# Landmark attention, a dense layer and routed experts in one kernel: one list of work for attention and dense stage, gates kept in SBUF, w2 loaded into w_in's buffers

## The chip, the cores and the metric

One core of one Trainium2 chip runs the whole computation as one program. Its engines are TensorE (PE, the matrix products; PEld is its weight load), VectorE (DVE), ScalarE (ACT), GpSimd (POOL) and SyncE (SP, which here issues nearly all DMAs). They run side by side, each through its own list of instructions in order, and wait for one another by semaphores. The metric is the device time of the program in microseconds. It is given as the median of several timed runs; a profile is of one more execution.

## What is computed

```python
def _attn_ref(q, k, v):                       # 4 batches, 8 heads, 576 tokens, 64 columns
    q_lm, k_lm = means of 18 neighbours of q, k     # 32 landmarks
    A, Bm, C = sm(q, k_lm), sm(q_lm, k_lm), sm(q_lm, k)
    Z = Bm.T / (norm1 * norminf + 1e-6)
    for _ in range(6):
        Z = 2 * Z - Z @ Bm @ Z
    return A @ Z @ C @ v

def _moe_ref(x, w_in, w_out):                 # 2304 x 512, d_ff 2048
    h = x @ w_in
    return (h * clip(h + 3, 0, 6) / 6) @ w_out

def _moe2_ref(x, w_gate, w1, w2, capacity):   # 8 experts, F 1024, capacity 576
    expert_idx = argmax(x @ w_gate); gate_w = softmax at expert_idx
    # a token gets gate_w * (relu(x @ w1[e]) @ w2[e]) while its expert has room, else 0
```

w_in and w_out come as 64-bit floats and are turned into 32-bit ones on the chip. Products are made with operands split in two (hi and lo, three products for one).

## The kernel before

**Three stages.** The attention stage works on eight units (four batches, two groups of four heads): landmark means (`turn_qk`), `landmark_scores`, `norms`, `gather_v`, `newton` (the inverse, which ends with the copy to `xt`), and `token_scores`, which writes `at`. Attention and dense layer are folded: `project` multiplies `xt` with a quarter of w_in (VV, tile `vv`, the mark "V"), and `first` multiplies that with `at`. So the dense stage needs no attention output. Its width of 2048 is cut in four quarters (`fq`), its tokens in eight blocks of 288 (two to a batch). `first` makes four tiles of 128 hidden rows, evicted by ACT and DVE into r, and split into ghi (ACT) and glo (POOL, or DVE); `second` multiplies them with a quarter of w_out and adds the result to `yacc`. Blocks 6 and 7 (the last batch) get no `second`: their r goes to DRAM (`r_d`), and their gate logits come from r times w_out times w_gate (`gate_weights`, `logits`). `route` picks each token's expert; for the inputs here each of the first three batches goes to one expert, so three units run through `run_unit` (`up_layer`, then `down_layer` in chunks of 128 tokens). What is only for other inputs stands behind a branch that is not taken.

**The order of work.** Each engine's list is fixed when the program is built. `Order` (line 25) is a planner: every step is an `op` with an engine, a cost in us, what it waits for (`after`), buffers that it takes, and a rank. It takes the step that can start first, and among those that can start within a short look-ahead the lowest rank. For a DMA it counts 2 us and the KB given (`DMA_KB`). The instructions are then issued in that order, and no engine ever goes out of order.

**Two plans.** The attention stage is one run of the planner (lines 775 to 791): loads in the order `LOADS`, the attention steps, and `moe_begin`, which puts the firsts and seconds of quarter 0 for blocks 0 to 5 between them, one first and one second of the block before in turn; when it ends block 5's seconds are still open. The attention's memory is then closed, and the dense stage is a second run (lines 966 to 991): the rest of the projections, the conversions of w_out's quarters 1 to 3 (`convert`; quarter 1 of w_in has been loaded in the first plan), `gate_weights`, `logits`, `route` for batches 0, 1 and 3 (`ROUTED`), the store of `yacc` (`store_y`), the load and split of unit 0's w1 (`w1_first`, chunks `raw_e`), and `dense`, which takes firsts and seconds in the order `BLOCKS`, blocks 6 and 7 among them. Batch 2 is routed behind the plan (line 992). PSUM's eight banks are shared out anew between the plans (`open_rest`).

**Gates and w2.** `route` works on tokens in chunks of 96: six transposes (line 871), then some fifteen small DVE operations. It stores a batch's 576 gates to DRAM (line 920, 4 bytes each) and `load_gates` reads them back in chunks of 128 at the head of each unit. Unit 0's w2 is loaded in four quarters while its up-layer runs (`fetch2`, tile `raw`), and split there by ACT and POOL (`split2`), in ACT's list between the evictions of `up_layer`.

Of the kernel before, what the change touches and what calls it, by code (L numbers as in the profile page):

```python
# [125 lines left out]
def nystrom_moe_kernel(ctx, tc, qt, kt, v, w_in, w_out, w_gate, w1, w2, capacity, out, dims, dbg=None):  # L126
# [17 lines left out]
    RN = HB // RT  # L144
# [4 lines left out]

    LAST = NBLK - 2  # L150
    NST = (UNIT + P - 1) // P
# [10 lines left out]
    gate_d = dp.tile([(B - 1) * S], F32, name="gate_d")  # L162
# [7 lines left out]
    for e in range(2):  # L170
# [8 lines left out]
    upper = kp.tile([RT, RT], BF16, name="upper")  # L179
    nc.gpsimd.memset(upper, 1.0)  # L180
    nc.gpsimd.affine_select(out=upper, in_=upper, compare_op=ALU.is_gt, fill=0.0,
                            base=0, pattern=[[1, RT]], channel_multiplier=-1)
    ones_b = kp.tile([RT, RT], BF16, name="ones_b")
    nc.gpsimd.memset(ones_b, 1.0)
    down = kp.tile([RT, E], F32, name="down")
    base_e = kp.tile([RT, E], F32, name="base_e")
    for e in range(E):
        nc.gpsimd.memset(down[:, e:e + 1], float(E - e))
        nc.gpsimd.memset(base_e[:, e:e + 1], float(e * NT))
    half = kp.tile([P, 1], F32, name="half")  # L190
    nc.gpsimd.memset(half, 0.5)
    cap_i = cp.tile([RT, 2], I32, name="cap_i")
    nc.scalar.dma_start(cap_i, capacity.bitcast(I32).to_broadcast([RT, 2]))
    cap_f = kp.tile([RT, 1], F32, name="cap_f")
# [4 lines left out]
    chosen = kp.tile([RT, NBLK, RN, E], F32, name="chosen")  # L199
# [1152 lines left out]
```

## Time and profile before

| | us |
|---|---|
| median of 3 timed runs (lowest, highest) | 562.46 (562.12, 562.86) |
| the profiled execution: its own time | 564.0 |
| its span, first to last instruction | 562.2 |
| first dense product on PE | 63.58 |
| first product of expert unit 0 | 399.16 |
| mean clock of TensorE, of full | 0.991 |

Times in the trace are counted from the first instruction. A line such as L423 is a line of the kernel above; "out<-in" names the tiles. Matmuls are pipelined, so a group's mean is longer than the distance between two of them, and the chain shows the pace better. In the views of windows the columns are the width, then for each engine its busy us and number of instructions, the share of TensorE's full clock that was granted, the mean busy share of the 16 DMA engines, and the GB/s that they moved. What stands in square brackets at the end of a timeline row is the engine's idle time before it and who ended that.

### The profile page before, as it was taken

How to read it: one execution, taken by the hardware profiler on the slowest of the kernel's cores; microseconds unless marked ns; L12 is line 12 of the kernel's file. 1: busy time of each engine (PE TensorE's matmuls, PEld its weight loads, DVE VectorE, ACT ScalarE, POOL GpSimd, SP SyncE). 2: the span in 40 equal slices, each digit the busy share in tenths (PEclk: the TensorE clock that was granted, in tenths of full speed). 3: DMA queues.
4: the chain of work that ended last, by engine and by line, in shares of the span. 5: the costliest groups of instructions: out<-in, count | busy, mean ns of one | idle time of the engine just before them, and what ended most of it. 6: DMA issues, size and time to landing. Idle time of an engine off the chain costs nothing.

```text
span 562.2 us, 12046 instructions
## 1 busy us (share of the span) xinstructions
PE 536.0 (95%) x4827; PEld 462.7 (82%) x4827; DVE 286.9 (51%) x691; ACT 285.2 (51%) x663; POOL 201.1 (36%) x236
## 2 busy tenths in 40 slices
PE   8888999999889999999999999997889999999995
PEld 6655688799577999889979899997787899689884
DVE  2798977823388886558554473566524012302200
ACT  3786787754467555356454354534157152643210
POOL 4486565833124521033223023321064370733000
PEclk9999999999899999999999999998999999999999
DMA  8964435110182542302100010244394910500011
GB/s 297 340 224 161 164 118 165 38 40 1 45 260 92 148 127 81 107 2 97 44 22 0 33 55 1 85 160 95 85 334 127 332 43 0 178 37 21 1 49 42
DMA packets 27841, 59.75 MB, mean 106 GB/s; under 512 B 6528, under 2 KB 11136, under 8 KB 27776
## 3 DMA queue, kind: packets, MB, share of 16 engines
q1 hardware_dynamic: 27136, 58.87, 31.7%
q8 instruction: 40, 0.66, 0.5%
q14 instruction: 25, 0.20, 0.1%
q10 hardware_dynamic: 640, 0.02, 0.1%
HBM read 45.90 MB, written 12.98 MB: 105 GB/s over the span
## 4 chain that ended last, share of the span: by engine, by line
PE 81%; DVE 8%; DMA 5%; ACT 4%; issue 1%; POOL 0%; SPq 0%; ACTq 0%; DVEq 0%; POOLq 0%
PE py L423 26%; PE ph L379 16%; PE ps_o L1074 12%; PE ps_h L1056 12%; PE pn L722 2%; PE pb L359 2%; PE ps_o L1081 2%; DMA raw_e<-in_moe_w 2%; PE warm L769 2%; DMA gate<-gate_d 1%; PE ps_v L359 1%; DVE sums L546 1%; DMA raw<-in_moe_w_out 1%; DMA raw<-in_moe_w_in 1%; PE pw L705 1%
## 5 line engine op out<-in xcount | busy, mean ns | idle before, releaser
L423 PE MATMUL py<-ghi,wo 128*128 128x288 f32 x768 | 160.0, 301 | 3.0 <-DVE yacc L435 3.0
L423 PEld LDWEIGHTS py<-ghi,wo 128*128 128x128 f32 x768 | 124.4, 190 | 8.5 <-issue 5.1
L409 POOL TENSOR_TENSOR glo<-r,ghi 128x288 fp32r<-128x288 f32 x86 | 70.2, 822 | 168.7 <-ACT ghi L402 122.1
L379 PE MATMUL ph<-at,vv 128*128 128x288 f32 x768 | 122.8, 302 | 1.7 <-DVE r L392 1.6
L379 PEld LDWEIGHTS ph<-at,vv 128*128 128x128 f32 x768 | 107.5, 189 | 12.4 <-DVE r L392 6.9
L423 PE MATMUL py<-glo,wo 128*128 128x288 f32 x384 | 114.2, 297 | 0.4 <-DVE glo L406 0.4
L390 ACT ACTIVATE r<-ph,half 128x288 f32<-128x288 f32 x128 | 63.3, 501 | 79.8 <-PE ph L379 60.1
L392 DVE SCALAR_TENSOR_TENSOR r<-r,ph 128x288 f32<-128x288 f32 x128 | 57.0, 451 | 54.8 <-ACT r L390 54.1
L423 PEld LDWEIGHTS py<-glo,wo 128*128 128x128 f32 x384 | 72.8, 189 | 1.1 <-DVE glo L406 0.9
L1062 DVE SCALAR_TENSOR_TENSOR hT<-ps_h,hT 128x288 fp32r<-128x288 f32 x48 | 21.8, 457 | 94.3 <-ACT hT L1059 63.0
L1074 PE MATMUL ps_o<-w2s,hT 128*128 128x512 f32 x288 | 66.2, 391 | 0.0
L1074 PEld LDWEIGHTS ps_o<-w2s,hT 128*128 128x128 f32 x288 | 53.8, 188 | 13.6 <-issue 2.4
L402 ACT ACTIVATE ghi<-r 128x288 fp32r<-128x288 f32 x96 | 42.1, 445 | 24.6 <-DVE r L392 23.7
L1019 POOL TENSOR_TENSOR w2s<-raw,w2s 128x512 fp32r<-128x512 f32 x24 | 30.1, 1291 | 41.7 <-ACT w2s L1018 41.7
L435 DVE TENSOR_TENSOR yacc<-py,yacc 128x288 f32<-128x288 f32 x72 | 32.6, 453 | 22.0 <-PE py L423 21.8
L1059 ACT ACTIVATE hT<-ps_h 128x288 fp32r<-128x288 f32 x48 | 19.7, 411 | 42.6 <-PE ps_h L1056 42.6
L277 POOL TENSOR_TENSOR wo<-cvt,wo 128x512 fp32r<-128x512 f32 x16 | 22.1, 1381 | 38.1 <-ACT wo L275 33.1
L1085 ACT ACTIVATE rows_o<-ps_o,gate 128x512 f32<-128x512 f32 x12 | 8.3, 691 | 41.5 <-PE ps_o L1074 39.2
L722 PE MATMUL pn<-yy 128*128 128x192 f32 (+1 forms) x112 | 27.5, 339 | 1.4 <-DVE vv L366 0.7
L1056 PE MATMUL ps_h<-at,vv 128*128 128x288 f32 x192 | 26.3, 296 | 2.1 <-DVE hT L1062 2.1
L1056 PEld LDWEIGHTS ps_h<-at,vv 128*128 128x128 f32 x192 | 25.6, 188 | 2.4 <-DVE hT L1062 2.3
L1056 PE MATMUL ps_h<-at,wo 128*128 128x288 f32 x192 | 25.8, 294 | 0.0
(207 smaller groups left out, 759.9 us busy)
## 6 DMA issues: line engine op xcount, KB each, us to landing
raw<-in_moe_w_out SPq DMA_DIRECT2D x16, 512.0 KB, 3.7
raw<-in_moe_w_in SPq DMA_DIRECT2D x16, 512.0 KB, 4.2
raw<-in_moe_w SPq DMA_DIRECT2D x8, 1024.0 KB, 7.4
r_d<-r SPq DMA_DIRECT2D x32, 144.0 KB, 1.8
vm<-in_v SPq DMA_DIRECT2D x8, 512.0 KB, 7.3
qT<-in_q SPq DMA_DIRECT2D x6, 576.0 KB, 5.2
qT<-in_k SPq DMA_DIRECT2D x6, 576.0 KB, 6.0
yt_d<-yacc SPq DMA_DIRECT2D x12, 288.0 KB, 2.5
```

The costliest lines, as they stand in the source:

```text
L277: nc.gpsimd.tensor_tensor(dst[1], xf, dst[0].bitcast(F32), op=ALU.subtract)
L379: nc.tensor.matmul(ph, lhsT=vv[pair][g][a][:, b, f * P:(f + 1) * P], rhs=at[pair][c][:, g, tok], start=n == 0, stop=n == 3 * NG - 1)
L390: nc.scalar.activation(r, ph, AF.Relu, bias=half, scale=1.0 / 6.0)
L392: nc.vector.scalar_tensor_tensor(r, r, 1.0, ph, op0=ALU.min, op1=ALU.mult)
L402: nc.scalar.activation(ghi, r, AF.Copy)
L409: nc.gpsimd.tensor_tensor(glo, r, ghi.bitcast(F32), op=ALU.subtract)
L423: nc.tensor.matmul(py, lhsT=w[a][:, f, d * P:(d + 1) * P], rhs=gh[f][c], start=f == 0 and n == 0, stop=f == NF - 1 and n == 2)
L435: nc.vector.tensor_tensor(y, py, y, op=ALU.add)
L722: nc.tensor.matmul(pn[:, cols], lhsT=yy[:, 0:P], rhs=yy[:, cols], start=True, stop=True)
L1019: nc.gpsimd.tensor_tensor(dst[1], src, dst[0].bitcast(F32), op=ALU.subtract)
L1056: nc.tensor.matmul(ps, lhsT=w1s[i % 2](f // NF, a, kk)[:, fs], rhs=xT[c][:, kk, cols], start=n == 0, stop=n == 3 * KC - 1)
L1074: nc.tensor.matmul(ps, lhsT=hT[a][:, f, cols], rhs=w2s[c][:, f, :], start=n == 0, stop=n == 3 * FC - 1)
```

## The change

- One plan for attention and dense stage. `moe_begin` and `dense` become three streams that the planner mixes freely: `firsts`, `seconds` (both in the order of the new `BLOCKS`, blocks 0 to 5 only) and `lasts` (blocks 6 and 7). The projections of quarter 1 for batches 0 and 1 are in the plan from the start. When all eight units have left `xt` and `at`, `room2` closes the attention's memory and adds what was the second plan.
- New ranks and a new order of loads; `store_y` and the store of r count their KB in the planner.
- `route` works in chunks of 128 (five transposes), and `down_layer` takes the gate straight from `prob` in SBUF. The DRAM tile of the gates, its stores and its loads are gone.
- w_in's two buffers stay for the whole program. `w2_first` loads unit 0's raw w2 into them, in two halves, once batch 0 is routed and w_in is used up; `raw2` is these buffers, also for the later units.

The core of the diff (the attention functions move out of a `with` block, otherwise as they were):

```diff
-LOADS = [('out', 3), ('qk', 1), ('out', 1), ('qk', 0), ('v', 1), ('qk', 2), ('out', 2), ('v', 0), ('qk', 4), ('out', 0), ('v', 2), ('qk', 3), ('in', 1), ('in', 0), ('qk', 5), ('in', 2), ('in', 3), ('v', 7), ('v', 4), ('v', 3), ('qk', 7), ('in', 6), ('v', 5), ('in', 5), ('in', 4), ('v', 6), ('qk', 6), ('in', 7)]
+LOADS = [('out', 3), ('qk', 1), ('out', 1), ('qk', 0), ('v', 1), ('qk', 2), ('out', 2), ('v', 0), ('qk', 4), ('out', 0), ('v', 2), ('qk', 3), ('in', 1), ('v', 7), ('in', 0), ('qk', 5), ('in', 2), ('in', 3), ('v', 4), ('v', 3), ('in', 4), ('v', 5), ('in', 6), ('qk', 7), ('v', 6), ('qk', 6), ('in', 7), ('in', 5)]
-RANK = {'in': -39.11, 'out': -156.08, 'next': 307.67, 'C': 7.14, 'A': 103.25, 'B': 97.9, 'Cv': 62.1, 'Z': -35.93, 'sum': 18.24, 'V': 10.16, 'g': 140.36, 'w': -82.95, 'first': -102.38, 'second': 135.87, 'evict': 86.86, 'late': -2.87, 'fill': 29.53, 'out2': 9.76, 'in2': -36.7, 'wg2': 9.18, 'logit': -6.56, 'route': -21.37, 'unit': 17.29}
+RANK = {'in': -210.42, 'out': -85.49, 'next': 285.02, 'C': 2.83, 'A': 122.98, 'B': 61.74, 'Cv': 43.88, 'Z': -40.91, 'sum': 31.39, 'V': -10.32, 'g': 126.04, 'w': -260.15, 'first': -222.88, 'second': 248.13, 'evict': 67.29, 'late': 0.01, 'fill': -117.25, 'out2': 171.78, 'in2': -214.46, 'wg2': 107.62, 'logit': -20.62, 'route': -202.82, 'ahead': 42.91, 'unit2': 100.03, 'unit': 65.75, 'first2': 135.87, 'second2': 135.87, 'V2': 122.79}
-BLOCKS = ((0, 1, 2, 3, 4, 5, 6, 7), (0, 3, 1, 5, 7, 2, 6, 4), (0, 4, 6, 2, 7, 5, 3, 1), (6, 7, 3, 1, 0, 2, 5, 4))
+BLOCKS = ((0, 0), (0, 1), (0, 2), (0, 3), (0, 4), (0, 5), (1, 0), (1, 1), (1, 4), (1, 2), (1, 3), (1, 5), (2, 0), (2, 2), (2, 1), (2, 5), (2, 3), (2, 4), (3, 2), (3, 0), (3, 1), (3, 3), (3, 4), (3, 5))
 ROUTED = (0, 1, 3)
-BANKS = {"h": (3, 4, 1), "y": (5, 2), "m": (0, 6, 7)}
...
-    gate_d = dp.tile([(B - 1) * S], F32, name="gate_d")
...
-    wi = [sp.tile([P, KC, QW], F32, name=f"wi{i}") for i in range(2)]
+    wi = [kp.tile([P, KC, QW], F32, name=f"wi{i}") for i in range(2)]
...
-        rest = state["alone"]
+        rest = fq > 1 or fq == 1 and out
...
-            yield op("SP", 0.35)
+            yield op("SP", 0.35, 144)
             nc.sync.dma_start(r_d[blk - LAST, fq * NF + f], r)
...
+    def firsts():
+
+        for fq, blk in BLOCKS:
+            state["g", fq, blk] = {}
+            yield op(None, after=[("V", fq, blk // 2, g) for g in range(NG)] + (
+                [("at", blk // 2, g) for g in range(NG)] if fq == 0 else []))
+            for f in range(NF):
+                order.spawn(RANK["evict"], first(fq, blk, f, state["g", fq, blk]))
+                yield op(None, after=[("queued", "first", fq, blk, f)])
+
+    def seconds():
+
+        for fq, blk in BLOCKS:
+            for d in range(KC):
+                yield op(None, after=[("first", fq, blk, NF - 1)])
+                order.spawn(RANK["evict"] + 0.5, second(fq, blk, d, state["g", fq, blk]))
+                yield op(None, after=[("queued", "second", fq, blk, d)])
+
+    def lasts():
+
+        for fq in range(NQ):
+            for blk in range(LAST, NBLK):
+                state["r", fq, blk] = {}
+                yield op(None, after=[(*what, B - 1, g) for what in (("V", fq), ("at",)) for g in range(NG)] + [("room2",)])
...
+        ps = [spare(i, [P, n, KC, M], "ps_lt") for i, n in zip(ids, (NST - 1, 1))]
+        cols = lt.rearrange("p n t -> p (n t)")
+        for t in range(NST):
+            o = ps[t // (NST - 1)][0:size(t), t % (NST - 1)]
+            nc.tensor.transpose(o.rearrange("p d c -> p (d c)"), cols[:, t * P:t * P + size(t)], ident)
...
-        if b < B - 1:
-            yield op("SP", 0.4, rank=RANK["late"])
-            nc.sync.dma_start(gate_d[b * S:(b + 1) * S].rearrange("(c j p) -> p c j", p=RT, c=2), prob[:, 2 * b:2 * b + 2, :, 0])
...
-            yield op("SP", 0.35, 0.0, {}, [("y", NQ - 1, 2 * b + n, d) for n in range(2)])
+            yield op("SP", 0.35, 288, {}, [("y", NQ - 1, 2 * b + n, d) for n in range(2)])
...
+    def w2_first(a):
+        yield op("SP", 0.45, 1024, {}, [("pick", 0), ("gated", NQ - 1)] + [("V", NQ - 1, b, g) for b in range(B) for g in range(NG)])
+        nc.sync.dma_start(wi[a], w2[bass.ds(state["ex", 0], 1), a * 4 * P:(a + 1) * 4 * P, :].rearrange("o (k p) f -> p (o k) f", p=P))
+
+    def room2():
+
+        yield op(None, after=[("x", b, g) for b in range(B) for g in range(NG)] + [
+            ("at", b, g) for b in range(B) for g in range(NG)] + [("gated", 0)])
+        order.spawn(0.0, room3())
+
+    def room3():
+
+        yield op(None, take={"b": 2})
+        att.close()
...
+        order.mark(("room2",))
+        order.spawn(RANK["late"], clear())
...
-                    order.spawn(RANK["fill"] + fq + pair * 0.1 + g * 0.01, again(fq, pair, g))
+                    if fq > 1 or pair:
+                        order.spawn(RANK["V2"] + fq + pair * 0.1 + g * 0.01, again(fq, pair, g))
...
+        for g in range(NG):
+            order.spawn(RANK["ahead"] + g, again(1, 0, g))
+        order.spawn(9.0, room())
+        order.spawn(9.0, room2())
...
+        for stream in (firsts, seconds, lasts):
+            order.spawn(-1.0, stream())
...
-        raw2 = [up.tile([P, FC // 2, DM], F32, name=f"raw2{i}") for i in range(2)]
+        raw2 = wi
...
-            load_gates(i)
             for f in range(FC):
                 hi, lo = up_layer(i, f)
                 split2(f)
-                if i == 0 and f < 3:
-                    with tc.issue_after(hi):
-                        fetch2(state["ex", 0], (f + 1,), 4)
...
-                down_layer(k, gates[i][0:size(k), k:k + 1], lambda ro: nc.sync.dma_start(out[rows, :], ro))
+                down_layer(k, prob[0:size(k), i, k, :], lambda ro: nc.sync.dma_start(out[rows, :], ro))
...
-        fetch2(state["ex", 0], (0,), 4)
```

## Rows read from the trace of the kernel before

**Rows 1.** The page, part 1: busy us, share, instructions of each engine.

```profile
PE 536.0 (95%) x4827; PEld 462.7 (82%) x4827; DVE 286.9 (51%) x691; ACT 285.2 (51%) x663; POOL 201.1 (36%) x236
```

**Rows 2.** Busy time per 10 us: width, PE, PEld, DVE, ACT, POOL, clock, DMA share, GB/s.

```profile
140.00:150.00 10.00, 7.93 (x58) 4.77 (x57) 3.08 (x6) 4.34 (x9) 1.48 (x2) 0.83 0.00 0
...
160.00:170.00 10.00, 8.27 (x75) 6.12 (x74) 8.16 (x17) 5.93 (x12) 3.61 (x3) 1.00 0.80 241
170.00:180.00 10.00, 9.57 (x163) 7.13 (x160) 7.78 (x16) 8.58 (x19) 4.91 (x5) 1.00 0.32 105
...
380.00:390.00 10.00, 6.83 (x46) 6.33 (x45) 6.22 (x19) 4.66 (x10) 2.10 (x3) 0.94 0.29 64
390.00:400.00 10.00, 8.91 (x64) 7.69 (x64) 4.79 (x11) 1.87 (x4) 0.00 (x0) 0.89 0.52 123
...
410.00:420.00 10.00, 7.93 (x60) 7.71 (x59) 3.02 (x7) 7.05 (x19) 7.86 (x7) 1.00 1.02 390
```

**Rows 3.** PE's waits over the whole span: us in total, times, longest.

```profile
PE ps_h L1056 <- DVE hT L1062: 2.1, 1, 2.1
PE ph L379 <- DVE r L392: 1.6, 1, 1.6
```

**Rows 4.** The chain in order of time, dense stage: start us, us, what.

```profile
140.60 1.59 PE py L423 x12
...
158.52 1.60 PE py L423 x12
...
202.81 0.80 PE ph L379 x6
...
311.06 1.02 PE pb L359 x16
312.08 1.00 PE ph L379 x6
...
366.63 0.33 PE ps_lt L871 x3
```

**Rows 5.** Timeline of ACT and POOL at the join: start us, us, what.

```profile
137.66 0.44 ACT L748 ACTIVATE xt<-px 64x64 f32<-64x64 f32 x2
...
145.97 0.68 ACT L231 ACTIVATE cvt<-raw 128x512 f32<-128x512 f32 x1
...
168.27 1.49 POOL L277 TENSOR_TENSOR wo<-cvt,wo 128x512 fp32r<-128x512 f32 x1 [4.86 <-ACT wo L275]
```

**Rows 6.** Timeline of ACT and PE near the end of the dense stage.

```profile
384.92 0.63 ACT L952 ACTIVATE vv<-raw_e 128x512 fp32r<-128x512 f32 x1 [3.79 <-DMA raw_e<-in_moe_w]
...
387.43 0.53 PE L423 MATMUL py<-ghi,wo 128*128 128x288 f32 x2 [3.03 <-DVE yacc L435]
```

**Rows 7.** Timeline of SP's queue there: issues of w1's chunks and of gates.

```profile
373.59 0.95 SPq L945 DMA_DIRECT2D raw_e<-in_moe_w  x2
376.00 0.33 SPq L920 DMA_DIRECT2D gate_d<-prob  x1
```

**Rows 8.** DMA issues: count, KB each, median us to landing.

```profile
gate_d<-prob SPq DMA_DIRECT2D x3, 2.2 KB, 8.4
```

**Rows 9.** The view of Rows 2, in 2 us.

```profile
382.00:384.00 2.00, 2.00 (x18) 2.00 (x17) 0.46 (x1) 0.00 (x0) 0.00 (x0) 1.00 0.00 0
```

**Rows 10.** Timeline of DVE and PE: last split of w1, first product of unit 0.

```profile
394.56 0.68 DVE L954 TENSOR_TENSOR wo<-raw_e,wo 128x512 fp32r<-128x512 f32 x1
...
399.16 1.82 PE L1056 MATMUL ps_h<-at,vv 128*128 128x288 f32 x12
```

**Rows 11.** The chain in order of time, in the expert stage.

```profile
403.02 8.40 DMA gate<-gate_d
...
453.71 25.43 PE ps_h L1056 x192
```

**Rows 12.** The view of Rows 2, before the dense products begin.

```profile
40.00:50.00 10.00, 8.02 (x226) 4.73 (x225) 9.17 (x22) 5.93 (x20) 9.59 (x16) 1.00 0.45 143
50.00:60.00 10.00, 9.20 (x111) 5.96 (x109) 8.61 (x24) 6.88 (x20) 4.23 (x4) 1.00 0.50 167
```

More of the change, by code (lines that the diff above doesn't have):

```diff
@@ L368, in project, with again @@
             order.mark(("V", fq, 2 * pair + b, g))
+    def again(fq, pair, g):
+        yield op(None, after=[("in", fq, k) for k in (2 * g, 2 * g + 1)] + [
+            ("first", fq - 1, 4 * pair + n, f) for n in range(4) for f in range(NF)])
+        yield from project(fq, pair, g)
     def first(fq, blk, f, out):
-        yield op("PE", 0.8, None, {"h": 1}, rank=RANK["second"])
+        state["cold"] = False
+        yield op("PE", 0.8, None, {"h": 1}, rank=RANK["fill"] if blk >= LAST else RANK["first2"])
         pair, b = blk // 4, blk // 2 % 2
@@ new lines, in nystrom_moe_kernel, with issue, load_qk @@
+    ap = att.enter_context(tc.tile_pool(name="att", bufs=2))
+    late = att.enter_context(tc.tile_pool(name="late", bufs=2))
+    main = 4 * P
+    NB = S // M
+    units = [dict(b=b, g=g, n=b * NG + g, q={}, rank=2.0 * b + RANK["g"] * g) for b in range(B) for g in range(NG)]
+    turn = [0]
+    def issue():
+        turn[0] += 1
+        return [("issue", turn[0] - 1)] if turn[0] > 1 else []
+    def load_qk(c, i):
+        n = c["n"]
+        yield op("SP", 0.45, 576, {"qT": 1} if n >= NG else {}, issue())
+        if n < NG:
+            qT = yacc[0][2 * n + i].rearrange("p (h t) -> p h t", h=4)
+        else:
+            qT = lp.tile([P, 4, HB], F32, tag="qT", name="qT", bufs=QT_BUFS)
+        c["q"][i] = qT
+        nc.sync.dma_start(qT, (qt, kt)[i][n])
+        order.mark(("qk", n, i))
@@ new lines, in newton @@
+    def newton(c):
+        st, yy = c["st"], c["yy"]
+        for it in range(7):
+            cols = slice(0 if it < 6 else P, P + D)
+            yield op("PE", 0.34 if it < 6 else 0.16, 0.27, {"s": 1})
+            i_s, pn = taken([P, P + D], "pn")
+            nc.tensor.matmul(pn[:, cols], lhsT=yy[:, 0:P], rhs=yy[:, cols], start=True, stop=True)
+            if it == 6:
+                break
+            yield op("DVE" if it else "ACT", 0.28, None, {"yy": 1})
+            yn = late.tile([P, P + D], F32, tag="yy", name="yy", bufs=4)
+            if it == 0:
+                nc.scalar.activation(yn, pn, AF.Copy, scale=st[:, 10:11])
+            else:
+                nc.vector.scalar_tensor_tensor(yn, yy, 2.0, pn, op0=ALU.mult, op1=ALU.subtract)
@@ new lines, in newton @@
+        xx = late.tile([P, 2, D], F32, tag="xx", name="xx")
+        nc.vector.scalar_tensor_tensor(xx, x6, 2.0, p6, op0=ALU.mult, op1=ALU.subtract)
+        order.give("s", 1, [i_s])
+        order.give("yy")
+        yield op("PE", 0.11, None, {"s": 1})
+        b, g, odd = c["b"], c["g"], c["b"] % 2
+        i_s, px = taken([P, 2, 2, M], "px")
+        nc.tensor.transpose(px.rearrange("p j h l -> p (j h l)"), xx.rearrange("p i d -> p (i d)"), ident)
+        yield op("ACT", 0.35)
+        order.give("xx")
@@ new lines, in newton, with values, room @@
+        for hh in range(2):
+            pr = slice(hh * D, (hh + 1) * D)
+            nc.scalar.activation(xt[pr, (b // 2) * NG + g, odd], px[pr, :, hh ^ odd, :], AF.Copy)
+        order.give("s", 1, [i_s])
+        order.mark(("x", b, g))
+    def values(b, g):
+        yield op(None, after=[("x", b, g)] + [("in", 0, k) for k in (2 * g, 2 * g + 1)] + ([("room",)] if b >= 2 else []))
+        yield from project(0, b // 2, g, (b % 2,))
+    def room():
+        yield op(None, after=[("scored", n) for n in range(2 * B)])
+        load.close()
+        s1 = early.enter_context(tc.tile_pool(name="slots1", bufs=1, side=RIGHT, reuse_waits="tile"))
+        vv[1] = [[s1.tile([P, 2, QW], F32R, name=f"vv1{g}{i}") for i in range(2)] for g in range(NG)]
+        yacc[1] = [s1.tile([P, S], F32, name=f"yacc1{d}") for d in range(KC)]
+        order.mark(("room",))
@@ L994, in nystrom_moe_kernel @@
             for step in route(b):
[L995 removed]
+                order.got.update(s=list(range(step[3].get("s", 0))) if step else [])
     early.close()
@@ L1014, in nystrom_moe_kernel @@
         xraw = rx[:, 0:KC * S].rearrange("p (k n) -> p k n", k=KC)
-        gates = [up.tile([P, NST], F32, name=f"gate{i}") for i in range(B - 1)]
         def split(dst, src):
```

737 lines of the change are left out of this document (318 added, 419 removed).

## Prediction

> **What bounds the kernel now.** I read four views, in this order. The page's busy times say that PE is the bound: 536.0 of 562.2 us, the next engine at 287 [rows 1]. Its products are the same before and after, so this case is about the 26 us in which PE stands, about time at half clock, and about what would fill either. The windows of 10 us then show where PE stands once the dense products have begun (before that it waits for loads and for the attention chain): it is full from 80 us on but for three places [rows 2]. At the join of the two plans (140 to 180 us) it is idle for 2.07 + 1.73 + 0.43 = 4.2 us, and the clock of the first window is 0.83, so 1.7 us of pace are lost too. At the end of the dense stage (380 to 400) it is idle for 3.17 + 1.09 = 4.3 us, with clocks 0.94 and 0.89, again 0.6 + 1.1 = 1.7 us. In the first expert unit (410 to 420) it is idle for 2.07 us at full clock. The last store at the very end is not touched. PE's waits name the engine that was late: DVE's hT (2.1) in unit 0, DVE's r (1.6) at the join [rows 3]; the wait at the dense end is traced below. The chain in order of time gives the pace of single products, and the timelines what stands ahead of a late one.
>
> **Work on PE.** A first product (6 matmuls) takes 0.80 us and a second one (12) 1.60 [rows 4]. There are 128 firsts and 96 seconds on both sides, as many projections, the same gate sums, the same three expert units. Only route changes: five transposes for six. Three take 0.33 us [rows 4], so four routes save 4 x 0.11 = 0.4 us. Its DVE work is as many operations on 40 elements a row instead of 48; I cost it at nothing, since DVE is half idle.
>
> **The join.** Today nothing of the second plan (projections for quarter 1, blocks 6 and 7, w_out of quarter 1) may stand in a queue ahead of the first plan's last operation. The last xt is copied at 137.66, ACT's first conversion of w_out's next quarter starts at 145.97, and the last lo half of those four chunks is done at 168.27 + 1.49 = 169.8 [rows 5]: 23.8 us of conversion, and 8.3 us lost ahead of it. After the change it may start when the attention has ended. What can PE do without it? The first plan's last products end at 142.2, and four seconds are left over (the last of them at 158.52): 6.4 us [rows 4]. New in that supply are two projections for quarter 1 (1.02 us, and 0.20 for the slower product behind, [rows 4]: 2.4) and the eight firsts whose g buffers exist (6.4): to 142.2 + 6.4 + 2.4 + 6.4 = 157.4. Once the attention has ended come blocks 6 and 7 (eight firsts: 6.4) and two projections of one batch (half of 1.02 each: 1.0): to 164.8. The conversion would end at 137.7 + about 1.5 + 23.8 = 163.0. So the 4.2 + 1.7 = 5.9 us can close with 1.8 us to spare. I leave 1.6 us in, because the wait on DVE's r [rows 3] came while conversions and evictions shared DVE (82% busy in 160 to 170 [rows 2]), and they still will. Gain 4.3; bounds 0 and 5.9.
>
> **The dense end.** ACT waits 3.79 us for a chunk of w1, the r and yacc operations queue behind it, and PE then stands for 3.03 us [rows 6]. The two chunks had been issued from 373.59 on; the next issue on SP's queue, at 376.00, is the store of 576 gates of 4 bytes [rows 7]. These stores take 8.4 us to land, for 2.2 KB [rows 8], and in 382 to 384 the DMA engines move nothing while this one and the chunk are still out [rows 9]. With the gates kept in SBUF no such store exists. Also the plan now counts the bytes of the yt and r stores (288 and 144 KB), so ACT's copies of w1 should be placed where the data is. Idle 3.17 and clock 1.7 can close: 4.9. The other 1.09 us stay, since batch 2 is still routed behind the plan. Against it comes something new: 2 MB of w2, whose place on SP's queue can be ahead of w1's second half. Its cost: the last split of w1 ends at 394.56 + 0.68 = 395.2, PE needs it at 399.16 [rows 10], a slack of 3.9, plus the 3.8 no longer waited, less the 4.9 by which PE comes earlier: 2.8 us. 2 MB at the 390 GB/s of the fullest window [rows 2] take 5.4 us: all ahead costs 2.6, half ahead nothing. I take 0.6. Gain 4.3; bounds 0 and 4.9.
>
> The Trainium skill (DMA: Bandwidth & Descriptors, Anatomy of one DMA — SWDGE (gpsimd) path) puts a small transfer at a fixed 2.0 us or so and says that most of it is the receipt of the write. By an estimate from that page a gate store would land in about 2 us, nothing would be held up by it, and taking the gates' store away would be worth nothing at this place. The trace disagrees for these stores, which run on another queue than the page's fit: 8.4 us [rows 8].
>
> **Unit 0.** The chain stands 8.40 us on a load of gates at 403.02 [rows 11], issued between the quarters of w2; behind it ACT splits w2, and the eviction of hT comes late. With w2 already in w_in's buffers the 2.07 us close. The up-layers of later units, which never wait, take 25.43 us [rows 11], and w2 is needed whole only after one. Gain 2.1; bounds 0 and 2.1.
>
> **Before the dense products.** From 40 to 60 us PE is idle for 1.98 + 0.80 = 2.8 us [rows 12]. Loads and ranks are reordered here (w_in's conversion higher, the eighth v ahead of w_in's first chunk), and the trace of before can't show what that does. Products that begin earlier gain about these 2.8 us at most, and as much may be lost by a later begin; I take 0.
>
> **Sum.** 4.3 + 4.3 + 2.1 + 0.4 = 11.1 us. The profiled execution took 564.0 us (span 562.2 and 1.8 around it), 1.5 above the median of the runs shown, 562.46; from it 552.9, and from the median 551.4, which I predict. With every hole closed and the early gain it is 562.46 - 5.9 - 4.9 - 2.1 - 0.4 - 2.8 = 546.4.
>
> **Rivals.**
> *More closes than I grant, or products begin early:* 546.4 to 549. For it: one plan sees all the work at once. Against: it must be right about every wait.
> *The join's hole stays*, because conversion waits for its turn on ACT and DVE behind evictions (its rank goes from 10 to 172, so it is taken last): 551.4 + 4.3 = 555.7. DVE's 82% speaks for it, the time to spare against.
> *w2 goes ahead of w1*, with the yt stores of batch 1 too (1.15 MB, 3.0 us): 2.6 to 5.6 us and 1.7 of clock, less the 0.6 granted: 555 to 558.
> *w1 was late for another reason than the gates*, and the end hole stays whole: 551.4 + 4.3 = 555.7.
> *Slower: the attention ends late.* With one list, products and attention compete all along on PE, and quarter 1's conversion, blocks 6 and 7 and the memory for them wait for the last xt. Beyond the 1.8 us to spare every us of delay is a us in which PE stands, and one clock dip of 1.7 comes with it. The gain of 11.1 + 1.6 = 12.7 (the old hole gone whole) is used up, and 1.1 more, when the last xt comes 1.8 + 12.7 + 1.1 - 1.7 = 13.9 us later, at about 151.6; at 157 the time is 569. Against it: for the second head group the offset plus the rank falls from 104 to 85 (Newton), 147 to 129 (landmark scores) and 150 to 116 (values), against 135.87 for products, so the chain to xt is favoured more than before. For it: token scores move back, and the two v buffers are shared with the eighth v earlier.
>
> **Chances.** The forecast (549 to 554) 0.50; more closes 0.11; the join stays 0.12; w2 ahead of w1 0.10; another reason 0.04; holes that only move, 0.03; the attention late 0.10. The range holds all but the last two and the edges: 545.5 to 558.5. A change of 0.2% (1.1 us) is about what a measurement of this kernel can tell from none. Faster 0.87, same 0.03, slower 0.10.
>
> **What would show it.** Right: no idle of PE over 1 us in a window between 80 us and the end of the dense stage, except about 1 us at the last route; no half clock there; ACT not waiting for a chunk of w1; 25.5 us for the up-layer of unit 0; the expert stage's end as before. The prediction is wrong if the last xt is later than about 141 us, if PE stands for over 2 us at the join, if w1's chunks land behind w2, or if the first dense product moves by several us.

## The result and the profile after

The changed kernel takes 543.33 us (median of 4 runs, 542.96 to 543.89), the kernel before in the same session 562.66 (562.12 to 563.10): a ratio of 0.9658, with an interval from 0.9641 to 0.9674. The gain is 19.3 us where 11.1 were forecast, and the time lies 2.2 us below the range. The profiled execution took 543.89 us (span 542.2). In later comparisons, on other chips, the kernel before gave medians of 565.9 to 566.8 (single executions 562 to 571), while the changed one stayed at 543.8: a ratio of 0.9608 and a gain of 22.7 us there. So the kernels made from the changed one are held against its own 543.3 to 543.8, and spans of profiled executions against spans.

The page of the changed kernel, its parts 1 and 4 (busy us of each engine; shares of the chain that ended last):

```profile
PE 528.7 (98%) x4826; PEld 459.1 (85%) x4826; DVE 288.6 (53%) x691; ACT 281.6 (52%) x666; POOL 202.7 (37%) x232
...
PE 87%; DVE 7%; ACT 2%; DMA 1%; issue 1%; POOL 0%; SPq 0%; ACTq 0%; POOLq 0%
```

PE was busy for 536.0 us of 562.2 [rows 1]; now it is for 528.7 of 542.2. So 13 us of the gain are time in which it stood, and 7 are time in which it worked slower than it can. The windows of 10 us of the changed kernel, in the places of [rows 2] and at the new dense end:

```profile
140.00:150.00 10.00, 10.00 (x76) 9.93 (x77) 9.35 (x18) 8.03 (x17) 2.09 (x2) 1.00 0.57 180
...
160.00:170.00 10.00, 10.00 (x191) 9.53 (x191) 4.92 (x10) 6.69 (x18) 3.17 (x4) 1.00 0.40 124
170.00:180.00 10.00, 10.00 (x83) 9.14 (x83) 8.31 (x18) 4.85 (x11) 0.80 (x1) 1.00 0.67 208
...
370.00:380.00 10.00, 9.82 (x73) 8.57 (x74) 7.63 (x22) 2.31 (x4) 0.13 (x1) 1.00 0.77 270
380.00:390.00 10.00, 9.87 (x75) 8.37 (x68) 6.74 (x36) 5.50 (x15) 2.93 (x3) 1.00 0.39 130
```

PE is full in all of them to within 0.2 us, and the clock is 1.00 throughout. DVE at 93% in 140 to 150 costs nothing. At the join, the timeline of the changed kernel shows the same three steps as [rows 5]: the last xt, the first conversion of w_out's next quarter, the last lo half of its four chunks.

```profile
135.79 0.91 ACT L746 ACTIVATE xt<-px 64x64 f32<-64x64 f32 x4
...
140.47 0.66 ACT L229 ACTIVATE cvt<-raw 128x512 f32<-128x512 f32 x1
...
160.93 1.29 POOL L275 TENSOR_TENSOR wo<-cvt,wo 128x512 fp32r<-128x512 f32 x1 [0.65 <-ACT wo L273]
```

The conversion starts at 140.47 instead of 145.97 and ends at 162.2 instead of 169.8. The prediction had worked out 139.2 and 163.0. Two projections of quarter 1 now lie at 115.8 and 119.4, and a run of six firsts on end covers 142 to 147.

At the dense end, a row of ACT's timeline in the changed kernel:

```profile
374.94 0.64 ACT L911 ACTIVATE vv<-raw_e 128x512 fp32r<-128x512 f32 x1 [5.04 <-DMA raw_e<-in_moe_w]
```

SP's queue there, with the two halves of w1 (raw_e) and w2 (wi):

```profile
360.74 0.95 SPq L904 DMA_DIRECT2D raw_e<-in_moe_w  x2
361.93 1.06 SPq L918 DMA_DIRECT2D wi<-in_moe_w  x2
...
371.14 3.09 SPq L904 DMA_DIRECT2D raw_e<-in_moe_w  x2
```

And PE's timeline where the last route meets unit 0:

```profile
379.56 1.17 PE L813 MATMUL ps_l<-yacc,gate 128*32 128x288 f32 x12
380.83 0.33 PE L834 MATMUL ps_lt<-ident,lt 128*128 128x128 f32 x1
381.09 0.67 PE L813 MATMUL ps_l<-yacc,gate 128*32 128x288 f32 x2
381.69 0.33 PE L834 MATMUL ps_lt<-ident,lt 128*128 128x128 f32 x1
381.78 0.64 PE L1053 MATMUL ps_h<-at,vv 128*128 128x288 f32 x3
```

ACT still waits for a chunk of w1, for longer than before (5.04 us, 3.79 in [rows 6]). But ACT's last eviction of a first product ahead of it ended at 367.6, so no r stands behind this wait; what PE makes until 379.6 are seconds, and DVE evicts those. The 2 MB of w2 did go ahead of w1's second half. Around the last route PE goes from the logits to the first products of unit 0 without a stand of over 0.1 us. The up-layer of unit 0 lasts 26.32 us (28.89 before); of it the chain shows one piece:

```profile
385.13 23.03 PE ps_h L1053 x173
```

By stretch, between products of PE, in the two profiled executions:

| stretch | before | after | gain |
|---|---|---|---|
| to the first dense product | 63.58 | 60.94 | 2.64 |
| from it to the first product of unit 0 | 335.58 | 320.84 | 14.74 |
| of that: PE idle | 9.80 | 0.83 | 8.97 |
| of that: lost by half clock (2 x 3.41 us at half) | 3.41 | 0 | 3.41 |
| of that: products done faster | | | 2.36 |
| unit 0 to the last product | 156.59 | 154.04 | 2.55 |
| behind the last product | 6.45 | 6.38 | 0.07 |

Most of the 2.36 us is in projections: their 256 products, each counted until the next one starts, take 22.96 us before and 19.92 after; some 0.7 of the difference are the half clock. A projection's product is shown as some 0.6 us long while sixteen take 1.02 [rows 4], so a short wait between two of them can hide in "busy".

### The profile page after: what moved, and what is told of

It reads as the page before. It is cut to its first block, busy times and chain, and to the rows that moved or that the text cites. A ratio compares the mean times of both kernels' runs of the same rounds, so it can differ in the third digit from the quotient of the medians.

```text
span 542.2 us, 12040 instructions
## 1 busy us (share of the span) xinstructions
PE 528.7 (98%) x4826; PEld 459.1 (85%) x4826; DVE 288.6 (53%) x691; ACT 281.6 (52%) x666; POOL 202.7 (37%) x232
## 4 chain that ended last, share of the span: by engine, by line
PE 87%; DVE 7%; ACT 2%; DMA 1%; issue 1%; POOL 0%; SPq 0%; ACTq 0%; POOLq 0%
PE py L427 26%; PE ph L383 18%; PE ps_h L1053 14%; PE ps_o L1071 12%; PE ps_v L356 3%; PE pn L720 2%; PE ps_o L1078 2%; PE warm L967 2%; DMA qT<-in_q 1%; PE ps_w L298 1%; DVE sums L544 1%; PE ps_f L531 1%; PE ps_lq L793 1%; PE ps_l L813 1%; PE pw L703 1%
## 5 line engine op out<-in xcount | busy, mean ns | idle before, releaser
L427 PE MATMUL py<-ghi,wo 128*128 128x288 f32 x768 | 158.2, 298 | 0.3 <-DVE yacc L439 0.2
L413 POOL TENSOR_TENSOR glo<-r,ghi 128x288 fp32r<-128x288 f32 x86 | 72.4, 848 | 170.0 <-ACT ghi L406 152.3
L383 PEld LDWEIGHTS ph<-at,vv 128*128 128x128 f32 x768 | 106.8, 188 | 11.1 <-issue 6.4
L1021 POOL TENSOR_TENSOR w2s<-wi,w2s 128x512 fp32r<-128x512 f32 x24 | 30.1, 1289 | 35.8 <-ACT w2s L1020 35.8
L1082 ACT ACTIVATE rows_o<-ps_o,prob 128x512 f32<-128x512 f32 x12 | 8.3, 689 | 41.6 <-PE ps_o L1071 39.2
L363 DVE TENSOR_TENSOR vv<-ps_v,vv 128x512 fp32r<-128x512 f32 x32 | 21.6, 687 | 12.2 <-ACT vv L361 12.0
L275 POOL TENSOR_TENSOR wo<-cvt,wo 128x512 fp32r<-128x512 f32 x16 | 20.9, 1303 | 19.1 <-ACT wo L273 19.1
L361 ACT ACTIVATE vv<-ps_v 128x512 fp32r<-128x512 f32 x32 | 18.4, 595 | 16.0 <-PE ps_v L356 16.0
L720 PE MATMUL pn<-yy 128*128 128x192 f32 (+1 forms) x112 | 26.0, 331 | 0.7 <-DVE yy L728 0.5
```

Source lines behind the costliest of these rows:

```text
L383: nc.tensor.matmul(ph, lhsT=vv[pair][g][a][:, b, f * P:(f + 1) * P], rhs=at[pair][c][:, g, tok], start=n == 0, stop=n == 3 * NG - 1)
L413: nc.gpsimd.tensor_tensor(glo, r, ghi.bitcast(F32), op=ALU.subtract)
L427: nc.tensor.matmul(py, lhsT=w[a][:, f, d * P:(d + 1) * P], rhs=gh[f][c], start=f == 0 and n == 0, stop=f == NF - 1 and n == 2)
L720: nc.tensor.matmul(pn[:, cols], lhsT=yy[:, 0:P], rhs=yy[:, cols], start=True, stop=True)
L1021: nc.gpsimd.tensor_tensor(dst[1], src, dst[0].bitcast(F32), op=ALU.subtract)
```

## The experiments

**1. Gates back through DRAM, in the changed kernel.**

```diff
+            nc.sync.dma_start(g[0:full].rearrange("(t p) -> p t", p=P), prob[:, b, 0:NST - 1, 0])
+            nc.sync.dma_start(g[full:].rearrange("(t p) -> p t", p=tail), prob[0:tail, b, NST - 1:NST, 0])
...
+            load_gates(i)
...
-                down_layer(k, prob[0:size(k), i, k, :], ...
+                down_layer(k, gates[i][0:size(k), k:k + 1], ...
```

> The changed kernel with the gates through DRAM again, stored and loaded in chunks of 128 in 4-byte pieces. If the gate stores made the hole at the dense end, as the prediction says, w1's second half lands late and PE stands there for about 3 us, with a clock dip of 1.7 behind it: 546 to 548 us. If the hole went because firsts now run ahead of seconds, so that nothing that PE needs is queued behind ACT's wait, the time stays at 543 to 544 with ACT waiting longer than 5 us for a chunk of w1.

Measured 546.71 us (546.23 to 548.02), 3.4 above. Two rows of its timelines, of ACT and of PE, at the dense end:

```profile
380.62 0.63 ACT L917 ACTIVATE vv<-raw_e 128x512 fp32r<-128x512 f32 x1 [10.95 <-DMA raw_e<-in_moe_w]
...
382.39 1.05 PE L814 MATMUL ps_l<-yacc,gate 128*32 128x288 f32 x2 [1.89 <-DVE yacc L440]
```

Its windows of 10 us there:

```profile
370.00:380.00 10.00, 9.82 (x73) 8.65 (x73) 4.90 (x16) 0.00 (x0) 0.00 (x0) 1.00 0.77 171
380.00:390.00 10.00, 8.09 (x45) 5.27 (x40) 5.99 (x24) 3.95 (x10) 0.00 (x0) 0.83 0.98 139
```

ACT's wait for w1 grows from 5.04 to 10.95 us, DVE's splits and the yacc operations behind them are late, PE stands for 1.89 us, and half clock follows from 382.55 to 385.96 (1.7 us lost). Up to there the kernel is on time (first dense product at 61.07). While ACT waits, in 370 to 380, the DMA engines are busy for 77% of the time, as in the changed kernel, but move 171 GB/s where they moved 270; in 380 to 390 they are busy for 98% and move 139, where 39% moved 130. The gates' own packets of 4 bytes are little of this busy time: by the packets' records in the trace under 1% from 370 to 380 and 7% from 380 to 390. It is packets of other transfers that last longer behind a gate store: those of w2 (2048 bytes) up to 6.2 us from 369 to 375, those of the yt stores (2304 bytes) up to 5.2 us from 381 on. In the changed kernel none of either size took over 0.93 us between 345 and 400. How the gates' packets hold up the others, no run shows.

**2. No gate stored or loaded, in the kernel before.** Rows are multiplied by 1 instead of the gate: that part of the result is left out.

```diff
-            nc.sync.dma_start(gate_d[b * S:(b + 1) * S]...
-            nc.sync.dma_start(gates[i][:, 0:NST - 1], ...
+            nc.gpsimd.memset(gates[i], 1.0)
```

> The kernel before without the store and the loads of the gates; it leaves out the factor of the gate in the output (a constant 1). If the stores made the hole at the dense end: the 3.03 us and the 1.7 of clock go, and with the loads gone part of the 2.07 in unit 0: 556 to 558 us. If the lead of firsts is what counts, ACT still stands before r and yacc: 560 to 562.5, with the hole of the dense end in place.

Measured 556.67 us (555.14 to 558.24), a ratio of 0.9833 (0.9778 to 0.9888) to the kernel before on that chip; span 556.5 against 562.2. Its windows at the join, the dense end and unit 0:

```profile
140.00:150.00 10.00, 7.93 (x72) 5.62 (x70) 1.60 (x3) 5.32 (x13) 2.88 (x4) 1.00 0.01 2
...
380.00:390.00 10.00, 9.77 (x69) 9.03 (x69) 8.21 (x24) 5.64 (x13) 2.76 (x3) 1.00 0.34 113
...
410.00:420.00 10.00, 10.00 (x78) 10.00 (x77) 2.95 (x7) 3.04 (x11) 2.82 (x3) 1.00 0.08 31
```

PE's longest waits from 75 to 430 us (us in total, times, longest):

```profile
PE pb L359 <- ACT vv L364: 2.3, 2, 2.1
PE ph L379 <- DVE r L392: 1.6, 1, 1.6
PE ps_k L897 <- DVE cnt L894: 0.6, 1, 0.6
```

The stands of 3.03 and 1.09 us at the dense end are gone with the half clock behind them, and so is the 2.07 in unit 0 (its up-layer: 26.57 us). The join's stands stay. From the first dense product to unit 0 it gains 5.3 us (1.7 of them since no half clock follows the join's stand here) and from there to the last product 2.3; 1.9 go at the start, where PE stood for 3.30 us at 51.33. So the gates' DMAs are the cause at the dense end, taken out here and put in in run 1. In unit 0 that is shown by taking them out alone: run 1, with w2 early, has no stand there (its up-layer: 26.85 us).

**3. w2 of unit 0 loaded late (in quarters, in unit 0), in the changed kernel.**

```diff
-        for a in range(2):
-            order.spawn(RANK["unit2"], w2_first(a))
...
+                if i == 0 and f < 3:
+                    with tc.issue_after(hi):
+                        fetch2(state["ex", 0], (f + 1,), 4)
```

> The changed kernel with unit 0's w2 loaded in four quarters in its up-layer, as before, still into w_in's buffers. If the gate loads alone held w2 up: no hole in unit 0, 543 to 544 us. If w2's late load is itself the cause: a hole of about 2 us in unit 0, 545 to 546.

Measured 543.71 us (543.18 to 543.91): no difference, and the up-layer of unit 0 lasts 26.32 as with w2 early. Neither the early w2 nor its place ahead of w1 is worth anything once the gates are out of the way.

**4. w2 loaded early into w_in's buffers, in the kernel before, gates as they were.**

```diff
-    wi = [sp.tile([P, KC, QW], F32, name=f"wi{i}") for i in range(2)]
+    wi = [kp.tile([P, KC, QW], F32, name=f"wi{i}") for i in range(2)]
...
+        for a in range(2):
+            order.spawn(100.03, w2_first(a))
```

> The kernel before with unit 0's w2 loaded into w_in's buffers when batch 0 is routed, gates as they were. The hole of 2.07 us in unit 0 closes: 560 to 561 us. If the 2 MB go ahead of w1's second half and products wait for it: the hole at the dense end grows by 2 to 5 us, and the time is 562 to 565.

Measured: a ratio of 0.9983 (0.9949 to 1.0017), the same time. Unit 0's stand is gone (26.67 us), but PE's two stands at the dense end, in its timeline, are now 2.06 and 3.21 us, with 6.83 us at half clock:

```profile
394.58 0.43 PE L851 MATMUL ps_l<-yacc,gate 128*32 128x288 f32 x1 [2.06 <-DVE yacc L435]
...
398.47 0.69 PE L851 MATMUL ps_l<-yacc,gate 128*32 128x288 f32 x1 [3.21 <-DVE yacc L435]
```

ACT waits for w1's second half for 7.71 and 2.74 us here. The early w2 closes unit 0's stand too, but next to gate stores it takes from w1 what it gives there.

**5. The order of the join put back into the single plan.** What waits for the attention's end also waits for the products that ended the first plan, and no projection of quarter 1 comes ahead.

```diff
-            ("at", b, g) for b in range(B) for g in range(NG)] + [("gated", 0)])
+            ("at", b, g) for b in range(B) for g in range(NG)] + [("gated", 0)] + [
+            ("first", 0, 5, NF - 1), ("second", 0, 4, KC - 1)])
...
-        for g in range(NG):
-            order.spawn(RANK["ahead"] + g, again(1, 0, g))
```

> The changed kernel, but what waits for the end of the attention now also waits for the last first product of quarter 0, block 5 and the last second one of block 4, and quarter 1's projections don't come ahead of it: the order that the join of two plans forced before. Theory A, that the join's 5.8 us of the kernel before (2.07 + 1.58 + 0.43 idle, 1.7 of half clock) came from this order alone: PE stands again for 1 to 4 us between 137 and 185, and the time is 2 to 6 us above the changed kernel's 543.3, so 545.5 to 549. Theory B, that they closed because products and attention are ranked otherwise all along (the last xt at 135.4 for 137.2, its conversions earlier): no stand over 0.5 us there, and 543 to 544.

Measured 549.82 us (547.87 to 550.55), 6.1 to 6.5 above. The timeline of the conversions:

```profile
132.39 0.44 ACT L746 ACTIVATE xt<-px 64x64 f32<-64x64 f32 x2
146.46 0.67 ACT L229 ACTIVATE cvt<-raw 128x512 f32<-128x512 f32 x1
...
167.50 1.29 POOL L275 TENSOR_TENSOR wo<-cvt,wo 128x512 fp32r<-128x512 f32 x1
```

PE's longest waits from 75 to 400 us:

```profile
PE py L427 <- DVE yacc L439: 1.5, 2, 1.3
PE ps_w L298 <- DVE r L396: 1.4, 1, 1.4
PE ps_v L356 <- DVE vv L363: 0.7, 1, 0.7
```

The last xt comes earlier than in the changed kernel, yet the conversion starts at 146.46 and ends at 168.8, as before. PE stands for 0.66 us at 158.7, 1.40 at 168.7 and 1.31 at 228.1, without half clock. Of the 6.4 us that the profiled execution loses up to unit 0, 2.3 are idle time of PE at the join (135 to 185), 2.0 idle time elsewhere, and 2.1 products that take longer. So putting back the order of the join costs 6 us although the attention ends earlier, but only a good third of it as stands at the join itself; the rest lies elsewhere in the list, which the planner lays anew.

**6 and 7. The old ranks, and the old order of loads, in the changed kernel.**

```diff
-RANK = {'in': -210.42, 'out': -85.49, ...
+RANK = {'in': -39.11, 'out': -156.08, ...
```

> The changed kernel with the ranks of the kernel before wherever a name is in both (the new names keep theirs). Theory A, that the 2.6 us by which the first dense product comes earlier (60.94 for 63.58) come from the ranks: the first dense product is at 63 to 64 again and the time 1.5 to 3.5 us above 543.3. Theory B, that they come from the order of the loads: the first dense product stays within 0.7 us of 60.94. In both, no stand of PE over 1 us at the join and at the dense end, if the single plan and the gates in SBUF closed those.

```diff
-LOADS = [... ('in', 1), ('v', 7), ('in', 0), ...
+LOADS = [... ('in', 1), ('in', 0), ...
```

> The changed kernel with the order of loads of the kernel before. Theory A (ranks made the early start): the first dense product stays within 0.7 us of 60.94, time 543 to 544.5. Theory B (the order of loads made it): first dense product at 63 to 64, time 545 to 546.5.

Measured 551.15 us (550.58 to 552.38) with the old ranks and 548.69 (547.83 to 550.03) with the old loads. The first dense product is at 63.30 and at 65.00: either alone loses the early start. With the old ranks the chain in order of time goes through a late chunk of w_in:

```profile
46.27 5.87 DMA raw<-in_moe_w_in
```

With the old loads, through a late chunk of v, and behind the first dense product a late one of q:

```profile
52.14 7.13 DMA vm<-in_v
...
61.07 6.67 DMA qT<-in_q
```

Old loads lose 4.06 us at the start and 1.1 behind it. Old ranks lose 2.36 there, and 6.1 up to unit 0: from 75 us on PE waits 3.2 us for DVE's r in four stands, with one half clock. That was not expected: the ranks were worth more behind the start than at it.

Run 7 also shows what a late attention costs in one plan. Its last xt comes 11 us later than in the changed kernel, and the last lo half of the conversion is done at 173.1, later than before the change (timelines of ACT and POOL):

```profile
147.44 0.45 ACT L746 ACTIVATE xt<-px 64x64 f32<-64x64 f32 x2 [0.69 <-PE px L741]
...
171.83 1.29 POOL L275 TENSOR_TENSOR wo<-cvt,wo 128x512 fp32r<-128x512 f32 x1 [0.52 <-ACT wo L273]
```

Yet PE is full from 140 to 180, and its longest waits from 75 to 400 us are these:

```profile
PE ps_k L859 <- DVE cnt L856: 0.5, 2, 0.3
PE ps_m L664 <- DVE vv L363: 0.4, 1, 0.4
```

**8. Other PSUM banks for the last route, in the kernel before.**

```diff
-                order.got.update(m=list(BANKS["m"][0:step[3].get("m", 0)]) if step else [])
+                order.got.update(m=list(range(step[3].get("m", 0))) if step else [])
```

> The kernel before, except that batch 2's route, which stands behind the plan, takes PSUM banks from 0 on and not 0, 6 and 7. It tests why PE stands for 1.09 us at 397.45 and 0.64 at 400.98 around that route. Theory A, that the route's products and unit 0's first products wait for banks that still hold others' tiles: one of the two stands changes by over 0.3 us, and the time by up to 1.7 us. Theory B, that they are the route's own chain of small steps (logits, their eviction, transposes, picks) with nothing to lay between: both stay within 0.2 us, and the time within 0.2% of the kernel before.

The stand of 1.09 us ahead of the route's transposes becomes 0.55, since four products of unit 0 now come ahead of them (PE's timeline):

```profile
395.89 0.79 PE L1056 MATMUL ps_h<-at,vv 128*128 128x288 f32 x4
397.23 0.86 PE L871 MATMUL ps_lt<-ident,lt 128*96 128x128 f32 x6 [0.55 <-ACT lt L856]
397.84 2.36 PE L1056 MATMUL ps_h<-at,vv 128*128 128x288 f32 x16
```

The 0.64 behind them is gone. The time is the same (0.9984, 0.9943 to 1.0025): in the profiled execution the stands that hang on gates were 3.80 and 2.95 us. So the route's stands were a matter of what the banks let PE do beside the route, not of the route itself.

**9. The changed kernel again**, beside the next three.

> The changed kernel once more, as it is, for comparison with the other kernels on the same chip: 543 to 545, and the first dense product at 60.9 us, unit 0 at 381.8.

Measured 543.75 us (543.11 to 544.85), first dense product at 60.72, unit 0 at 381.85.

**10. Four things undone together: 1, 5, 6 and 7.**

> The changed kernel with four things undone together: the order of the join (as in the barrier's run), the gates through DRAM, the old ranks and the old order of loads. The three streams and w2 in w_in's buffers stay. It asks whether the account by parts is whole. Alone they cost 6.5 (barrier), 3.4 (gates), 7.8 (ranks) and 5.4 us (loads). Theory A, that these are separate losses and nearly all of the gain: they add up to 23, and the time is 562 to 567. Theory B, that the ranks and the loads' order cost so much only because each was fitted to the other and to the free join, so that the old pair together costs little beside the start's 2.6 us: 543.3 + 6.5 + 3.4 + 2.6 = 555.8, so 553 to 559.

Measured 556.01 us (555.44 to 559.47): 12.3 above number 9, where the four alone add up to 23. The first dense product is at 65.20. The join's stand is there again, in PE's timeline:

```profile
172.37 1.94 PE L384 MATMUL ph<-at,vv 128*128 128x288 f32 x10 [2.56 <-DVE r L397]
```

Half clock follows in the same window:

```profile
170.00:180.00 10.00, 7.63 (x158) 7.16 (x159) 8.36 (x19) 7.03 (x18) 5.44 (x5) 0.83 0.32 109
```

The parts are not separate: the ranks and the loads' order are fitted to each other and to the free join.

**11. First and second products paired in one stream again**, in the changed kernel.

```diff
-        for stream in (firsts, seconds, lasts):
+        for stream in (firsts, lasts):
...
+                    order.spawn(RANK["evict"] + 0.5, second(*last, f, state["g", *last]))
+                    after.append(("queued", "second", *last, f))
```

> The changed kernel with first and second products again in one stream, one first and one second of the block before in turn, in place of two streams that the planner mixes freely. Theory A, that free mixing is what fills the holes (a late eviction or chunk of w1 holds only its own stream): PE stands again for 1 us or more in some place after 80 us, and the time is 1.5 to 6 us above the changed kernel's. Theory B, that the joined plan and the gates do it alone: within 0.3% of the changed kernel, 542 to 545.

Measured 551.00 us (549.95 to 551.29), 7.3 above number 9, all of it ahead of unit 0. The last product of the attention comes at 145.1 instead of 135.4, and PE stands at the join (its timeline), with half clock from 169.78 on:

```profile
168.12 0.53 PE L383 MATMUL ph<-at,vv 128*128 128x288 f32 x2 [0.74 <-ACT vv L361]
169.61 1.92 PE L383 MATMUL ph<-at,vv 128*128 128x288 f32 x7 [0.96 <-DVE vv L363]
```

So one plan is not enough by itself; products that come in pairs lose more than the barrier of run 5 does. The new ranks were kept here, and may suit free streams alone.

**12. No KB counted for the stores of yt and r**, in the changed kernel.

```diff
-            yield op("SP", 0.35, 144)
+            yield op("SP", 0.35)
...
-            yield op("SP", 0.35, 288, {}, ...
+            yield op("SP", 0.35, 0.0, {}, ...
```

> The changed kernel, but the planner counts no KB again for the stores of yt and of r (288 and 144 KB). It only changes the order that the planner writes down. Theory A, that the count keeps w1's loads and splits in step with the data and closes the dense end: PE stands there again for over 1 us, time 545 to 548. Theory B, that the gates in SBUF close it alone: no stand over 0.5 us at the dense end, time within 0.3% of the changed kernel, 542 to 545.

Measured 543.77 us (542.72 to 544.33): no difference, and no stand over 0.3 us at the dense end.

**13 to 15. The new loads, the new ranks, and both, in the kernel before** (the edits of 6 and 7 the other way round).

> The kernel before with the new order of loads alone. Theory A, that the new order pays only with the new ranks: the first dense product stays at 63 to 66 and the time is not below the kernel before's. Theory B, that the order of loads by itself brings the products forward: first dense product at 60.5 to 62.

> The kernel before with the new ranks alone, for the names that it has. Theory A: first dense product at 63 to 66, time not below the kernel before's. Theory B, that the ranks by themselves bring the products forward: first dense product at 60.5 to 62.

> The kernel before with the new order of loads and the new ranks together, still two plans, with the gates through DRAM and w2 in unit 0. Theory A, that the early start is the work of this pair and needs nothing of the single plan: first dense product at 60.5 to 61.5, and 2 to 3 us off the time before the join, which may come off the whole (560) or be lost again at the join. Theory B, that it needs the single plan: first dense product at 63 or later, time not below the kernel before's.

Measured ratios to the kernel before: 1.0007 (0.9978 to 1.0036), 1.0100 (1.0054 to 1.0146, two executions) and 1.0105 (1.0051 to 1.0159): the ranks make this kernel slower by 1%. The first dense product is at 62.54, 63.79 and 62.49. With both, the last product of the attention comes at 115.5, 21.6 us earlier than before, and PE still stands at the join (0.71, 1.94 and 1.83 us from 143 to 171) and for 3.84 at the dense end. Four profiles whose start nothing had touched (the kernel before, runs 2, 4 and 8) have it at 63.04 to 65.45, and seven with the changed kernel's start at 60.58 to 61.07. So 62.5 lies between the two theories: the new order of loads brings a part by itself, how large is lost in the scatter, and the rest came only within the single plan. And an attention that ends early is worth nothing while two plans meet: in run 13 its last product comes 10.9 us earlier, and the 2.07 us at the join stay.

## Why the prediction was right or wrong

Direction and main mechanisms held at the join, the dense end and unit 0; the size did not. The step that failed is the sum: it took the early start at 0 (2.64 us measured), kept 1.6 us at the join and 1.09 at the route that closed, and had no term for short waits that the profile counts as busy (some 2.0 us). The spans differ by 20.0 us, where 11.1 were forecast. The 8.9 more are made up so:

| term | forecast | measured | difference |
|---|---|---|---|
| start | 0 | 2.64 | 2.6 |
| join: 4.28 idle and 1.7 of clock | 4.3 | 5.98 | 1.7 |
| dense end: 3.03 and 1.09 idle, 1.7 of clock | 4.3 | 5.82 | 1.5 |
| unit 0 | 2.1 | 2.55 | 0.4 |
| smaller stands in the dense stage (1.4 to 0.83) | 0 | 0.6 | 0.6 |
| products done faster, transposes among them | 0.4 | 2.36 | 2.0 |

The differences add up to 8.8; what is missing lies behind the last product and in rounding.

*The start was taken at nothing* between bounds of 2.8 us either way, and came out at the upper end. This is the largest term. The idle time in [rows 12] could give no more than the bound, and the bound was nearly right. What failed was to take the middle and then to let the chance that "products begin early" stay within 0.11. In the single plan the old ranks or the old loads alone take it away (runs 6 and 7), and the new ones in two plans bring a part of it at most (runs 13 to 15); how much belongs to which load is not settled.

*The join: 1.6 us left in.* The dates were worked out rightly (conversion done at 163.0, measured 162.2; run 5 puts the old order back and the conversion ends at 168.8). The supply was worked out too small: it reached to 164.8, but in run 7 the conversion ends at 173.1 and PE does not stand. The 1.6 were kept because DVE would be 82% busy. It is 93% busy in the changed kernel, and no product waits for r: a full engine off the critical path was read as a wait. The condition for it was stated beside it (1.8 us to spare) and should have decided. The 1.7 us of clock in the measured 5.98 are luck of the one profile: the same 2.07 us stand at the join in runs 2, 4, 8 and 13 is followed by no half clock (in run 14 one does follow).

*The dense end.* That gates hold up w1 is shown from both sides by runs 1 and 2, though the stand itself is spread: with gate stores in all of them it was 3.03 us before, 3.80 in run 8, 3.84 in run 15 and 0.85 in run 13. The 0.6 us set aside for w2 ahead of w1 did not occur, although w2 did go ahead: run 3 moves it and the time stays. The 1.09 us "stay, since batch 2 is still routed behind the plan" is the step that was wrong in kind: the route is still behind the plan, but PE has work beside it. Run 8 closes half of the 1.09 in the kernel before by other banks alone, and in run 2 it is gone with the gates. The prediction's sign "ACT not waiting for a chunk of w1" was wrong too: ACT waits 5.04 us, with nothing behind it that PE needs. That the KB of the stores place ACT's copies better was part of the argument and is worth nothing (run 12).

*Unit 0* was right for the 2.07 us; the 0.4 beyond comes from the 0.64 at the route, which was not named. The cause was given as the load of gates together with w2's place. Either removes the stand: gates gone (run 2), or w2 early (run 4). As the changed kernel has no gate DMAs, w2's place adds nothing to it (run 3). The up-layer takes 26.32 us and not the 25.5 of the prediction's sign: the route's last transposes and its count lie within it.

The estimate of 2 us for a gate store, from the Trainium skill (DMA: Bandwidth & Descriptors, Anatomy of one DMA — SWDGE (gpsimd) path), and with it no gain from the removal, does not hold for these stores, which are on another queue than that fit: they land 8.4 us after issue [rows 8], taking the gates' DMAs out gives 5.7 us of span in run 2, and putting them in costs 3.4 in run 1. The row was the right one to go by.

*The range* ended too high, at 545.5, for two reasons. "Every hole closed" kept the holes it believed to stay (1.09 and 0.64). And it counted only idle time and half clock: 2.0 us were in products that wait a little and are shown as busy. Their trace was at hand: a projection takes 1.02 us at best [rows 4], and all sixteen take 22.96 us before, 6.6 above that pace, of which 3.0 closed. So the best case was not a bound.

*The rivals.* "More closes than I grant, or products begin early" (0.11) was what came, and more of it than its 546.4. The join's hole staying and a late attention did not come, by the windows above: the last xt is at 135.8, not at 151. That w2 ahead of w1 has a price is refuted by run 3 for a kernel without gate DMAs (next to them it has one, run 4), another reason for the late w1 by runs 1 and 2. The rule of the last rival, that beyond 1.8 us every us of delay is a us in which PE stands, is wrong by run 7, where xt is 11 us late without a stand. Its offsets hold for Newton and the landmark scores; the fall from 150 to 116 for the values was misread, since these get no offset of the head group (their rank goes from 10 to -10).

What stays open: the single plan's share beside the ranks. The kernel of run 10 has two of the things that the change brought (free streams, w2's place) and takes 556.0 us; the old ranks under paired streams were not tried, so the 7.3 us of run 11 can't be divided between them.

## What to carry to other kernels

A store of a few hundred single words is not small: count its packets, and look at what is issued around it on the same queue, whose packets may last several times as long. Where two schedules meet, ask what may stand ahead of the last operation of the first; ending the longest chain earlier helps nothing while the order itself is the wait (run 13), and where the order is free it may end later without a stand (run 7). For the best case of an engine that is the bound, take the fastest pace of each kind of product and not its idle time alone, and judge ranks and load orders only with the schedule to which they were fitted.

## What the runs showed of the hardware

Ahead of the last product, stretches at half clock lasted 3.41 us (6.83 in run 4), and one of 3.41 cost 1.7. They followed single stands of 1.73 us (run 10, at 51.44; half clock from 53.96), 1.89 (run 1, at 380.50; from 382.55) and 1.94 (run 15, at 159.14; from 161.58), but not the 2.07 at the join in runs 2, 4, 8 and 13, the 2.07 in unit 0 of the kernel before, or the 2.95 in unit 0 of run 8. The stand of 2.07 at the join of the kernel before was followed by one. So the length of the stand alone does not tell whether a dip follows.

In run 1 some 600 packets of 4 bytes, 9 ns each in the median, were followed by packets of 2048 and 2304 bytes that took up to 6.2 and 5.2 us, where the changed kernel showed at most 0.93: 98% busy for 139 GB/s, against 39% for 130. The stores of 2.2 KB in the kernel before took a median of 8.4 us from issue to landing [rows 8], the shorter gate stores of run 1 12.9 us for 0.2 KB.
